# Soft-capped attention into soft-routed experts: k as plain fp32 transfers, w1 in whole rows, one raw V buffer

## The chip, the cores and the metric

The kernel runs on one core of a Trainium2 chip. The metric is the device time of one execution in microseconds; several executions give a median. The core has a matmul engine (TensorE, PE in the profile), a vector engine (VectorE, DVE), an activation engine (ScalarE, ACT), a general one (GpSimd, POOL) and SyncE (SP), which here only issues transfers. Matmuls write to PSUM, a small memory beside the working memory SBUF. Transfers between the chip's main memory and SBUF run on sixteen DMA engines; those that GpSimd issues show in queue q0, those of SyncE in q1.

## What is computed

Attention over 8 batches of 12 heads, 448 tokens of 64 elements each, with a soft cap on the scores, feeds a layer of 8 experts with 4 slots each.

```python
scores = scale * np.matmul(q, k.transpose(0, 1, 3, 2))
scores = cap * np.tanh(scores / cap)
attn = np.exp(scores - max); attn = attn / (sum + 1e-09)
x = (attn @ v), heads side by side           # (3584, 768)
logits = x @ phi                             # phi: (768, 32)
d = softmax of logits over the tokens
slot_input = d.T @ x                         # 8 experts x 4 slots x 768
h = np.maximum(slot_input[e] @ w1[e], 0.0)   # w1[e]: (768, 1024)
slot_out[e] = h @ w2[e]                      # w2[e]: (1024, 768)
out = (softmax of logits over the slots) @ slot_out
```

q, k, v, w1 and w2 are fp32 in main memory: 11 MB each for q, k and v, 25 MB for each of the weights.

## The kernel before

**Quads.** The attention goes in 24 quads Q of four heads each, three to a batch. A quad has two pairs n; the two heads h of a pair lie in the two halves of the 128 partitions. The 448 tokens of a head are seven columns of 64, so that token 7p + c is row p of column c. A head's keys make three and a half blocks of 128; the half blocks of both heads of a pair form one "mixed" tile. So a quad has 14 score tiles of 128 keys by 448 queries (`TILES`), made in six chunks (`CHUNKS`).

**A quad's steps**, by the names that the plan uses:
- `L`, `X`: q and k are loaded by GpSimd's queue, 224 KB each, with the cast from fp32 to bf16 in the transfer (`load`, L394), into two buffers each.
- `LV`, `XV`: V is loaded as fp32 by SyncE's queue in four transfers (`load_v`, L401) into one of two buffers `vraw`. `VC` casts it on GpSimd to `vb` (L406); `VS` writes a scaled copy `vw` on VectorE (L409). Both have two buffers.
- `T`, `C`: TensorE turns q and k by transposes of 64 columns (`turn`, L464), VectorE copies them out of PSUM (L470, L473), and the keys of the mixed tile into a block-diagonal `km` (L479).
- `SC`, `TH`: score matmuls (L494 mixed, L497) and the tanh on ScalarE (L507).
- `EX`: the exponential of eight tiles on ScalarE (L515). The six others are made on VectorE as a sum of four terms, `PH` (L528).
- `PV`: the products with V (`pv_mms`; L537, L540, L544), `NR` the division by the sums (L576, L577), `TX`, `CX` the turn of the result (L588, L592) for the logits.

Each quarter of the queries is 128 wide but the last, which is 64. The second head of a pair takes its queries in another order than the first, with the last column ahead, so that its odd quarter comes at the front. In the kernel before, the turned q holds eight columns, the last one twice, and each head reads seven of them. The mixed tile reads the seven of the first head's order for both; its products with V are then 130 wide, for both heads at once, but for the odd quarter, which VectorE first copies out for both heads into a block-diagonal tile `mt` (`MT`, L521).

**Weights.** While the attention runs, GpSimd's queue also loads w1 (32 parts of 384 KB) and w2 (32 parts), cast to bf16. All of w1 and the first `KEPT = 6` parts of w2 stay in SBUF. The other 26 parts of w2 go to a scratch in main memory (`w2d`) and are loaded again by SyncE once the attention gives its buffers free (`w2t`, L863).

**The order** of every engine's work is written out ahead by a list scheduler, `Plan`. It knows for each step an engine, an estimated duration (`COST`), the steps that it waits for and a due time, which the tables `DUE` and `HOLD` shift by name; the transfers are engines of their own, `DMA` for GpSimd's queue and `DMV` for SyncE's. Engines in `strict` take their steps in order of due time alone. The parts of the weights are spaced evenly over the plan. Each engine carries out its list in order and waits where an operand or a buffer isn't ready.

**After the attention** come the last batch's logits (to L855), the first layer (L886), the second layer (L917) in two halves, and the output, 11 MB, from L952 on.

Of the kernel before, what the change touches and what calls it, by code (L numbers as in the profile page):

```python
# [34 lines left out]
MIXED = slice(2, 8, 5)  # L35
# [7 lines left out]
ND_LAST = 4  # L43
FULL, ROWS, COLS, QUARTERS = range(4)
# [5 lines left out]
DUE = {"C0k": -10345, "C0q": -334861, "CAk": -123110, "CAq": -67932, "CE": -38879, "CN": -191711, "CS": -129158,  # L50
# [7 lines left out]
HOLD = {"C0q": 995, "CAk": 880, "CAq": 166, "CE": 267, "CN": 1500, "CS": 655, "CW": 848, "CX": 780, "Cq": 538, "ED":  # L58
# [5 lines left out]
COST = dict(quad=9000, lat=200, dma=4000, form=90, sc=100, scm=200, act=0.833, act0=70, ts=0.265, ts0=70,  # L64
            pvf=31, mixed=190, mtail=62, turn=430, xturn=410, copy=610, norm=830, vcast=1060, vscale=340, mcopy=220, kdiag=300,
            issue=800, load=1400, part=2050, same=300)


class Plan:
# [11 lines left out]
    def build(self):  # L81
# [11 lines left out]
        for Q in range(1, NQ):  # L93
            for n, nm in enumerate("kq"):
                t0 = Q * T - (2600, 1800)[n]
                op(("L", nm, Q), "POOL", C["issue"], [("T", nm, Q - 2)], t0 - 1.3 * T)
                op(("X", nm, Q), "DMA", C["load"], [("L", nm, Q)], t0 - 1.3 * T)
                op(("T", nm, Q), "PE", C["turn"] + 60 * n, [("X", nm, Q)], t0, take=True, form=(COLS, COLS))
                op(("C", nm, Q), "DVE", C["copy"] + (C["kdiag"], 90)[n], [("T", nm, Q), ("SC", Q - 2, nc - 1)], t0 + 400,
                   give=("T", nm, Q))  # L100
        for Q in range(NQ):
# [16 lines left out]
            op(("LV", Q), "SP", 1600, [("VC", Q - 2), ("VS", Q - 2)], t0 - 1.5 * T)  # L118
# [20 lines left out]
            op(("MT", Q), "DVE", C["mcopy"], [("EX", Q, 0), ("PV", Q - 2, "a1"), ("PV", Q - 2, "d")], te - 1, port=True)  # L139
            op(("PV", Q, "a0"), "PE", 24 * C["pvf"], [("EX", Q, 0)] + vs, te, take=True)  # L140
            op(("PV", Q, "a1"), "PE", C["mixed"] + C["mtail"], [("PV", Q, "a0"), ("MT", Q)], te + 1)
# [3 lines left out]
            op(("PV", Q, "d"), "PE", C["mixed"] + C["mtail"], [("MT", Q)] + vs, td - 10, take=True)  # L145
# [42 lines left out]
    def order(self):  # L188
# [3 lines left out]
        strict = ("ACT", "DMA", "DMV", "SP")  # L192
# [57 lines left out]
def kernel(  # L250
# [26 lines left out]
    KEPT = 6  # L277
# [14 lines left out]
    wide = consts.tile([P, 3 * P], BF16, name="ones")  # L292
    ones = wide[:, 0:P]
# [6 lines left out]
    pool.memset(wide[:, P:3 * P], 1.0)  # L300
# [26 lines left out]
    def load_w1(e, jh, fh):  # L327
# [10 lines left out]
    wjobs = [(load_w1, e, jh, fh) for e in range(E) for jh in range(2) for fh in range(2)]  # L338
# [12 lines left out]
    for nm in ("ld", "vr0", "qk0", "vr1", "ea0", "qk1", "ed0", "vb0", "ea1", "tm", "ed1", "vb1"):  # L351
        homes[nm] = att.enter_context(tc.tile_pool(name=nm, bufs=1))
# [4 lines left out]
    vraw = [homes[f"vr{n}"].tile([P, 2, SLOTS, DH], F32, name=f"vraw{n}") for n in range(2)]  # L357
# [3 lines left out]
    mt = [homes[f"vb{n}"].tile([P, 2, P], BF16, name=f"mt{n}") for n in range(2)]  # L361
# [6 lines left out]
    for t in (*mt, *km):  # L368
        dve.memset(t, 0.0)
# [27 lines left out]

    def load_v(Q):
        at = vraw[Q % 2].rearrange("p n (h t) d -> p n h (t d)", h=2)
# [5 lines left out]
    def vcast(Q):  # L405
        pool.tensor_copy(vb[Q % 2][:, :, :, 0:DH], vraw[Q % 2])  # L406

    def vscale(Q):
        dve.tensor_scalar(vw[Q % 2][:, :, 0:DH], vraw[Q % 2][:, 1, :, :], w_low, None, ALU.mult)  # L409

    first = {}
    TURN = {"k": [0, 4, 1, 5, 2, 6, 3], "q": [NT - 1] + list(range(NT))}
# [17 lines left out]
    def new_qkT(nm, Q):  # L430
        qkT[nm, Q] = homes[f"qk{Q % 2}"].tile([P, 2, (NT - 1 if nm == "k" else NT + 1), HP], BF16, name=nm + "T",
                                               tag=nm + "T", bufs=1)
        return qkT[nm, Q]
# [6 lines left out]
    def first_turn(nm, n, x0, x1, bank, at0):  # L440
        for x in range(x0, x1):
            for h in range(2):
                r = slice(h * HP, h * HP + HP)
                pe.transpose(bank[r, at0 + x - x0, :], casts[nm, n][r, TURN[nm][x], :], ident[r, r])

# [9 lines left out]
    def t0(nm):  # L455
        banks0[nm] = xbank(bank_of["T0", nm], [P, len(TURN[nm]), HP], BF16, name=nm + "p0")
        first_turn(nm, 1, 0, len(TURN[nm]), banks0[nm], 0)

    def turn(nm, Q):
        src = raws.pop((nm, Q))  # L460
        ps = xbank(bank_of["T", nm, Q], [P, 2, len(TURN[nm]), HP], BF16, name=nm + "ps")
        for x, c in enumerate(TURN[nm]):
            for h in range(2):
                pe.transpose(ps[h * HP:h * HP + HP, :, x, :], src[:, h, c * DH:(c + 1) * DH], ident)  # L464
# [23 lines left out]
    def qk_chunk(Q, s):  # L488
        for u in range(CHUNKS[s]):
# [3 lines left out]
            if h is None:  # L493
                pe.matmul(dst, km[Q % 2][:, n, :], qT[:, 1:NT + 1], start=True, stop=True)  # L494
            else:
                r = slice(h * HP, h * HP + HP)
                pe.matmul(dst, kT[r, 2 * t:2 * t + 2, :], qT[r, 1 - h:NT + 1 - h], start=True, stop=True)  # L497
# [19 lines left out]
    def mixed_tails(Q):  # L517

        for h in range(2):
            r = slice(h * HP, h * HP + HP)  # L520
            dve.tensor_copy(mt[Q % 2][r, :, r], rows(ea[Q % RQ])[r, MIXED, TAIL:S])  # L521

# [8 lines left out]
    def pv_mms(Q, dst, buf, vt, tiles, u0, begin=False, end=False):  # L531
        for g in range(NG):
            for x in tiles:
                n, h, t = TILES[x]
                q0 = (x - u0) * ROW + (g * P if not h else g * P + HP if g < NF else -HP)
                if h is not None:
                    pe.matmul(dst[:, 2 * g + h if g < NF else 2 * g, :], buf[:, q0:q0 + P], vt[:, 5 * h + t, :],  # L537
                              start=begin, stop=end, skip_group_check=True)
                elif g < NF:
                    pe.matmul(dst[:, 2 * g:2 * g + 2, :], buf[:, q0:q0 + P], vt[:, 3:5, :], start=begin,  # L540
                              stop=end, skip_group_check=True)
                else:
                    for h in range(2):
                        pe.matmul(dst[:, 2 * g, :], mt[Q % 2][:, n, :], vt[:, 3 + h, :], start=False, stop=end,  # L544
                                  skip_group_check=True)
                begin = False
# [4 lines left out]
    def pv(Q, what):  # L551
# [7 lines left out]
        if what == "a0":  # L559
            pv_mms(Q, dst, a, va, of(0, 0, NA), 0, begin=True)  # L560
        elif what == "a1":
            pv_mms(Q, dst, a, va, of(0, 0, NA, True), 0, end=True)
        elif what == "d":
            pv_mms(Q, dst, a, vd, of(1, 0, NA, True), 0, begin=True)
        elif what == "e":
            pv_mms(Q, dst, d, vd, of(1, NA + nd, NQT), NA)
        else:
            i = int(what[1])
            pv_mms(Q, dst, term_home(Q, i), vd if TERMS[i][1] == 1.0 else vw[Q % 2], range(NA, NA + nd), NA,
# [123 lines left out]
    def busy(n, home, by=None):  # L693
        by = ones if by is None else by
        if home.shape[-1] > P:
            for _ in range(n // 3):
                pe.matmul(home, ones, wide, start=True, stop=True)
# [7 lines left out]
        "C0": lambda nm: first_copy(nm, 1, 0, len(TURN[nm]), banks0.pop(nm), 0, dve),  # L705
        "L": load, "T": turn, "C": turned, "SC": qk_chunk, "TH": tanh_chunk, "LV": load_v,
        "VC": vcast, "VS": vscale, "MT": mixed_tails, "PH": term, "PV": pv, "EX": exp_tiles, "TX": x_turn, "CX": x_turned,
# [8 lines left out]

    load_first()
    load_v(0)
    for nm in "kq":
        load(nm, 1)  # L720
# [337 lines left out]
```

## Time and profile before

| | us |
|---|---|
| median of three runs | 301.25 |
| lowest and highest | 299.21, 301.88 |
| the profiled execution | 302.47 |
| its span, first to last instruction | 300.7 |

| engine | busy us | share of the span |
|---|---|---|
| TensorE | 257.6 | 86% |
| ScalarE | 234.9 | 78% |
| VectorE | 215.4 | 72% |
| GpSimd | 127.9 | 43% |

A group's row in the profile shows the line, the engine, the operation, the tiles written and read with their shapes, the count, the busy time, the mean of one instruction in ns, and behind the bar the idle time of the engine just before, with what ended it. Matmuls overlap each other, so that TensorE's busy time says little of its room. A queue's share is the time of its packets against sixteen engines over the stretch; packets of two queues can overlap, so shares add to more than 1. GB/s counts bytes written, and a cast from fp32 to bf16 writes half of what it reads.

### The profile page before, as it was taken

The numbers are of one execution on the slowest core, as the hardware profiler recorded it, in microseconds if no ns is written. First come the engines' busy times: TensorE is split into PE (matmuls) and PEld (weight loads), VectorE is DVE, ScalarE is ACT, GpSimd is POOL, SyncE is SP. The second block draws the span as 40 slices with busy tenths as digits, with TensorE's granted clock in tenths as the row PEclk, the third lists the DMA queues.
The fourth block names the chain that finished last, engine by engine and source line by source line (L and its number), as shares of the span: only waits on it lengthen the run. The fifth ranks groups of instructions, "written<-read, shape, count | busy, mean of one in ns | idle before, by whom it ended". The sixth has DMA issues, their size and how long they took to land.

```text
span 300.7 us, 11856 instructions
## 1 busy us (share of the span) xinstructions
PE 257.6 (86%) x5206; PEld 189.6 (63%) x5206; DVE 215.4 (72%) x465; ACT 234.9 (78%) x207; POOL 127.9 (43%) x188
## 2 busy tenths in 40 slices
PE   4789999499979999998998989897999989997610
PEld 4367678367766777677775767676677767543300
DVE  3378999179876987898687869875698786257730
ACT  2699999379986999899897989898799994236610
POOL 4644936536650765356634663476062200300000
PEclk9999999779997999999999999999799999999975
DMA  7978999999999999999999999999999799978995
GB/s 148 191 108 178 187 220 208 224 214 218 222 224 211 217 224 225 213 214 222 223 216 211 219 223 216 217 207 209 206 160 215 197 322 305 402 277 323 413 412 231
DMA packets 65203, 69.70 MB, mean 232 GB/s; under 512 B 4992, under 2 KB 60416, under 8 KB 65152
## 3 DMA queue, kind: packets, MB, share of 16 engines
q0 software_dynamic: 42992, 35.77, 75.9%
q1 hardware_dynamic: 22000, 32.94, 33.7%
q8 instruction: 41, 0.67, 0.8%
q10 hardware_dynamic: 160, 0.23, 0.3%
q14 instruction: 10, 0.08, 0.1%
HBM read 93.68 MB, written 21.23 MB: 382 GB/s over the span
## 4 chain that ended last, share of the span: by engine, by line
PE 55%; DMA 15%; ACT 12%; issue 6%; DVE 5%; SPq 2%; POOL 1%; DVEq 0%; ACTq 0%; POOLq 0%
PE pv L537 21%; PE sc L497 9%; DMA w1b<-in_moe_w_dram 8%; ACT exa L515 5%; ACT exa L507 3%; PE qps L464 3%; ACT exd L507 3%; PE sc L494 3%; PE kps L464 3%; PE xps L588 3%; DMA vraw<-in_v_dram 2%; PE pv L540 2%; DMA raw<-in_q_dram 2%; DMA out_dram<-ob 2%; PE so_ps L917 2%
## 5 line engine op out<-in xcount | busy, mean ns | idle before, releaser
L507 ACT ACTIVATE exa<-sc 128x1344 f16<-128x1344 f32 (+1 forms) x72 | 82.7, 1175 | 13.5 <-PE sc L497 9.1
L515 ACT ACTIVATE exa<-exa 128x3584 bf16<-128x3584 f16 x24 | 76.9, 3202 | 0.0
L507 ACT ACTIVATE exd<-sc 128x896 f16<-128x896 f32 x72 | 64.5, 924 | 12.0 <-PE sc L497 11.9
L528 DVE TENSOR_SCALAR term<-exd 128x2688 uint16<-128x2688 f16 (+1 forms) x72 | 62.0, 877 | 1.6 <-PE pv L537 1.2
L537 PEld LDWEIGHTS <-term 128*128 128x128 bf16 x1704 | 56.4, 97 | 8.0 <-issue 4.6
L497 PE MATMUL sc<-qT,kT 64*128 64x448 bf16 x288 | 51.2, 376 | 2.5 <-ACT exa L507 0.9
L537 PE MATMUL pv<-vb,term 128*128 128x65 bf16 x1136 | 43.2, 194 | 0.6 <-DVE term L528 0.3
L394 POOL DMA_DIRECT2D qb<-in_q_dram x23 | 17.3, 754 | 45.3 <-PE sc L497 32.7
L394 POOL DMA_DIRECT2D kb<-in_k_dram x23 | 18.2, 790 | 38.4 <-PE sc L497 34.2
L577 DVE TENSOR_TENSOR xq<-pv,rec 128x448 bf16<-128x448 f32 (+2 forms) x49 | 30.1, 615 | 1.7
L331 POOL DMA_DIRECT2D w1b<-in_moe_w_dram x32 | 26.5, 829 | 8.8 <-DMA w1b<-in_moe_w_dram 6.5
L406 POOL CAST vb<-vraw 128x1024 bf16<-128x1024 f32 x24 | 26.5, 1106 | 7.5 <-issue 4.1
L537 PE MATMUL pv<-vb,exa 128*128 128x65 bf16 x576 | 24.0, 200 | 3.0 <-issue 2.4
L537 PEld LDWEIGHTS <-exa 128*128 128x128 bf16 x576 | 21.5, 102 | 4.6 <-issue 3.0
L537 PE MATMUL pv<-vw,exd 128*128 128x65 bf16 x568 | 22.4, 196 | 2.0 <-issue 2.0
L629 POOL COPY e<-E 128x512 bf16<-128x512 bf16 x9 | 5.8, 641 | 42.2 <-ACT E L822 18.2
L473 DVE COPY qT<-qps 128x1024 bf16<-128x1024 bf16 x23 | 15.7, 684 | 10.1 <-PE qps L464 10.0
L537 PE MATMUL pv<-vw,term 128*128 128x65 bf16 x568 | 21.7, 193 | 1.2 <-issue 1.2
L335 POOL DMA_DIRECT2D w2d<-in_moe_w_dram x26 | 21.8, 853 | 0.0
L537 PEld LDWEIGHTS <-exd 128*128 128x128 bf16 x576 | 19.7, 99 | 3.1 <-issue 2.2
L528 DVE TENSOR_SCALAR exd<-exd 128x2688 uint16<-128x2688 f16 (+1 forms) x24 | 20.8, 868 | 0.8
L497 PEld LDWEIGHTS <-kT 64*128 64x128 bf16 x288 | 12.8, 94 | 13.3 <-issue 4.9
(143 smaller groups left out, 377.7 us busy)
## 6 DMA issues: line engine op xcount, KB each, us to landing
w1b<-in_moe_w_dram POOLq DMA_DIRECT2D x32, 384.0 KB, 14.2
w2d<-in_moe_w_dram POOLq DMA_DIRECT2D x26, 384.0 KB, 12.1
w2t<-w2d SPq DMA_DIRECT2D x26, 384.0 KB, 6.0
out_dram<-ob SPq DMA_DIRECT2D x9, 768.0 KB, 8.6
vraw<-in_v_dram SPq DMA_DIRECT2D x48, 128.0 KB, 6.5
kb<-in_k_dram POOLq DMA_DIRECT2D x23, 224.0 KB, 10.0
qb<-in_q_dram POOLq DMA_DIRECT2D x23, 224.0 KB, 10.2
vraw<-in_v_dram SPq DMA_DIRECT2D x48, 96.0 KB, 6.5
```

Source lines behind the costliest of these rows:

```text
L331: pool.dma_start(out=w1b[e][:, js, fs], in_=w1r[:, e, js, fs])
L335: pool.dma_start(out=dst, in_=bass.AP(tensor=src.tensor, offset=src.offset + half * HD, ap=[[D, P], [F * D, 4], [1, HD]]))
L394: pool.dma_start(out=t, in_=bass.AP(tensor=srcs[nm].tensor, offset=quad_at(Q), ap=[[NT * DH, P], [2 * S * DH, 2], [1, NT * DH]]))
L406: pool.tensor_copy(vb[Q % 2][:, :, :, 0:DH], vraw[Q % 2])
L464: pe.transpose(ps[h * HP:h * HP + HP, :, x, :], src[:, h, c * DH:(c + 1) * DH], ident)
L473: dve.tensor_copy(new_qkT(nm, Q), ps)
L497: pe.matmul(dst, kT[r, 2 * t:2 * t + 2, :], qT[r, 1 - h:NT + 1 - h], start=True, stop=True)
L507: act.activation(quad_ex(Q, u0, u0 + w).bitcast(F16), ring(Q, s)[:, 0:w, 0:S], ACT.Tanh, scale=qk_scale / cap)
L515: act.activation(t, t.bitcast(F16), ACT.Exp, scale=cap)
L528: dve.tensor_scalar(rows(term_home(Q, i))[:, 0:nd, 0:S].bitcast(U16), quad_ex(Q, NA, NA + nd).bitcast(F16), octaves * 128, base[i], ALU.mu ...
L537: pe.matmul(dst[:, 2 * g + h if g < NF else 2 * g, :], buf[:, q0:q0 + P], vt[:, 5 * h + t, :], start=begin, stop=end, skip_group_check=True)
L577: dve.tensor_tensor(xq[Q][:, s0:s1, n, :], ps[:, s0:s1, 0:DH], rec.to_broadcast([P, s1 - s0, DH]), op=ALU.mult)
```

## The change

Five things change together, and the plan is made anew with other tables.

1. k is loaded by SyncE as plain fp32 (448 KB) into one buffer `kraw`, and VectorE casts it into one buffer `kcast` (new steps `LK`, `XK`, `KC`). The load of quad Q waits for the cast of Q-1; the cast of Q waits for the turn of Q-1.
2. w1 comes in 24 parts of 512 KB, two blocks of 128 rows in their whole length of 1024, where it came in 32 parts of 384 KB, three blocks in half their length.
3. The second head's queries are turned in their own order, so that the turned q has seven columns and 14 transposes where it had 16. The mixed tile now holds the two heads' queries in different orders; its products with V are made per head, eight of ordinary width, and `mt` with its copies goes.
4. One buffer `vraw` for V in place of two: the load of quad Q waits for the casts of Q-1, where it waited for those of Q-2.
5. Eight parts of w2 stay in SBUF and 24 are reloaded. The room comes from the V buffer, `mt` and the wide tile of ones.

The plan's steps on `SP` and `DMV` are no longer strict, the weights' parts get their own durations, and they are spread over one quad more.

```diff
+    op(("LK", Q), "SP", 400, [("KC", Q - 1)], t0 - 1.3 * T)
+    op(("XK", Q), "DMV", C["load"], [("LK", Q)], t0 - 1.3 * T)
+    op(("KC", Q), KCAST, C["kcast"] if KCAST == "DVE" else 950, [("XK", Q), ("T", nm, Q - 1)], t0 - 0.5 * T, port=True)
...
-            op(("LV", Q), "SP", 1600, [("VC", Q - 2), ("VS", Q - 2)], t0 - 1.5 * T)
+            op(("LV", Q), "SP", 1600, [("VC", Q - 1), ("VS", Q - 1)], t0 - 1.5 * T)
...
-            op(("MT", Q), "DVE", C["mcopy"], [("EX", Q, 0), ("PV", Q - 2, "a1"), ("PV", Q - 2, "d")], te - 1, port=True)
...
-            t = 3000 + k * (NQ * T - 2 * T) / self.parts
+            t = 3000 + k * (NQ * T - T) / self.parts
             op(("W", k), "POOL", C["issue"], (), t, after=t)
-            op(("XW", k), "DMA", C["part"], [("W", k)], t)
+            op(("XW", k), "DMA", C["part1"] if k < 24 else C["part2"], [("W", k)], t)
...
-        strict = ("ACT", "DMA", "DMV", "SP")
+        strict = ("ACT", "DMA")
...
-    KEPT = 6
+    KEPT = 8
...
-        js, fs = slice(3 * jh, 3 * jh + 3), slice(512 * fh, 512 * fh + 512)
-        pool.dma_start(out=w1b[e][:, js, fs], in_=w1r[:, e, js, fs])
+        js = slice(2 * jh, 2 * jh + 2)
+        pool.dma_start(out=w1b[e][:, js, :], in_=w1r[:, e, js, :])
...
+    def load_k(Q):
+        sp.dma_start(out=kraw, in_=bass.AP(tensor=k.tensor, offset=quad_at(Q),
+                                           ap=[[NT * DH, P], [2 * S * DH, 2], [1, NT * DH]]))
+
+    def cast_k(Q):
+        (dve if KCAST == "DVE" else pool).tensor_copy(kcast, kraw)
+        raws["k", Q] = kcast
...
-    TURN = {"k": [0, 4, 1, 5, 2, 6, 3], "q": [NT - 1] + list(range(NT))}
+    TURN = {"k": [[0, 4, 1, 5, 2, 6, 3]] * 2, "q": [[*range(NT)], [NT - 1, *range(NT - 1)]]}
...
-                pe.matmul(dst, km[Q % 2][:, n, :], qT[:, 1:NT + 1], start=True, stop=True)
+                pe.matmul(dst, km[Q % 2][:, n, :], qT, start=True, stop=True)
...
+                n, a, t = TILES[x]
+                for h in range(2) if a is None else (a,):
+                    q0 = (x - u0) * ROW + (g * P if not h else g * P + HP if g < NF else -HP)
+                    pe.matmul(dst[:, 2 * g + h if g < NF else 2 * g, :], buf[:, q0:q0 + P],
+                              vt[:, 3 + h if a is None else 5 * h + t, :],
                               start=begin, stop=end, skip_group_check=True)
...
     load_first()
+    load_k(1)
     load_v(0)
-    for nm in "kq":
-        load(nm, 1)
+    load("q", 1)
```

More of the change, by code (lines that the diff above doesn't have):

```diff
@@ L43 @@
 ND_LAST = 4
+KCAST = "DVE"
 FULL, ROWS, COLS, QUARTERS = range(4)
@@ L48 @@
 PH = len(TERMS)
-DUE = {"C0k": -10345, "C0q": -334861, "CAk": -123110, "CAq": -67932, "CE": -38879, "CN": -191711, "CS": -129158,
[7 rows of a table removed]
-HOLD = {"C0q": 995, "CAk": 880, "CAq": 166, "CE": 267, "CN": 1500, "CS": 655, "CW": 848, "CX": 780, "Cq": 538, "ED":
[5 rows of a table removed]
-COST = dict(quad=9000, lat=200, dma=4000, form=90, sc=100, scm=200, act=0.833, act0=70, ts=0.265, ts0=70,
-            pvf=31, mixed=190, mtail=62, turn=430, xturn=410, copy=610, norm=830, vcast=1060, vscale=340, mcopy=220, kdiag=300,
-            issue=800, load=1400, part=2050, same=300)
+DUE = {"C0k": -50037, "C0q": -404649, "CAk": -142919, "CAq": -143270, "CE": -32285, "CN": -365487, "CS": -113014,
[7 rows of a table added]
+HOLD = {"C0k": 1500, "C0q": 1052, "CAk": 720, "CAq": 52, "CE": 739, "CN": 697, "CW": 223, "Cq": 749, "ED": 1313,
[3 rows of a table added]
+COST = dict(quad=9000, lat=200, dma=3000, form=90, sc=100, scm=200, act=0.833, act0=70, ts=0.265, ts0=70,
+            pvf=31, turn=430, xturn=410, copy=610, norm=830, vcast=1060, vscale=340, kcast=540, kdiag=300,
+            issue=800, load=1400, part1=2740, part2=2530, same=300)
 class Plan:
@@ L95, in build @@
                 t0 = Q * T - (2600, 1800)[n]
[L96 to L99, printed above, removed]
+                if nm == "k":
+                    op(("LK", Q), "SP", 400, [("KC", Q - 1)], t0 - 1.3 * T)
+                    op(("XK", Q), "DMV", C["load"], [("LK", Q)], t0 - 1.3 * T)
+                    op(("KC", Q), KCAST, C["kcast"] if KCAST == "DVE" else 950, [("XK", Q), ("T", nm, Q - 1)], t0 - 0.5 * T, port=True)
+                else:
+                    op(("L", nm, Q), "POOL", C["issue"], [("T", nm, Q - 2)], t0 - 1.3 * T)
+                    op(("X", nm, Q), "DMA", C["load"], [("L", nm, Q)], t0 - 1.3 * T)
+                op(("T", nm, Q), "PE", C["turn"], [("X", nm, Q), ("KC", Q)][1 - n:2 - n], t0, take=True, form=(COLS, COLS))
+                op(("C", nm, Q), "DVE", C["copy"] + (C["kdiag"], 0)[n], [("T", nm, Q), ("SC", Q - 2, nc - 1)], t0 + 400,
                    give=("T", nm, Q))
@@ L144, in build @@
             td = t0 + T + 1200
[L145 removed]
+            op(("PV", Q, "d"), "PE", 8 * C["pvf"], [("EX", Q, 0)] + vs, td - 10, take=True)
             for i in range(PH):
@@ L290 @@
     psT = ctx.enter_context(tc.tile_pool(name="psT", bufs=1, space=PSUM))
-    wide = consts.tile([P, 3 * P], BF16, name="ones")
-    ones = wide[:, 0:P]
+    ones = consts.tile([P, NS], BF16, name="ones")
     dve.memset(ones, 1.0)
@@ L356 @@
     terms_of = [homes["tm"].tile([P, ND * ROW], BF16, name=f"term{n}") for n in range(RP)]
-    vraw = [homes[f"vr{n}"].tile([P, 2, SLOTS, DH], F32, name=f"vraw{n}") for n in range(2)]
+    kraw = homes["ld"].tile([P, 2, S], F32, name="kraw")
+    kcast = homes["ld"].tile([P, 2, S], BF16, name="kcast")
+    vraw = homes["vr"].tile([P, 2, SLOTS, DH], F32, name="vraw")
     vb = [homes[f"vb{n}"].tile([P, 2, SLOTS, W], BF16, name=f"vb{n}") for n in range(2)]
@@ L851 @@
     for a in range(0, P, NS):
-        pe.matmul(junk[a:a + NS, :], ones[:, 0:NS], wide, start=True, stop=True,
+        pe.matmul(junk[a:a + NS, :], ones, w2b[:, 0, 0, :], start=True, stop=True,
                   skip_group_check=True)
```

91 lines of the change are left out of this document (35 added, 56 removed), and 22 rows, old and new, of tables (DUE, HOLD).

## The prediction

> **What bounds the kernel now.** I read the windows first, to see which stretch the time is in; then ScalarE's timeline and its waits, for what the long stretch lacks; then the transfer queues of the same stretch, and the chain.
>
> The kernel handles 24 quads (four heads each). The eight-tile exponentials of ScalarE (L515), one per quad, are a good ruler:
>
> ```profile
> 15.96 3.20 ACT L515 ACTIVATE exa<-exa 128x3584 bf16<-128x3584 f16 x1
> 42.79 3.20 ACT L515 ACTIVATE exa<-exa 128x3584 bf16<-128x3584 f16 x1
> 60.81 0.92 ACT L507 ACTIVATE exd<-sc 128x896 f16<-128x896 f32 x1 [5.54 <-PE sc L497]
> 245.68 3.20 ACT L515 ACTIVATE exa<-exa 128x3584 bf16<-128x3584 f16 x1
> ```
>
> ```profile
> core 0: us, PE busy (x) PEld busy (x) DVE busy (x) ACT busy (x) POOL busy (x), PEclk, DMA share, GB/s
> 15.96:42.79 26.83, 25.69 (x526) 19.42 (x525) 23.57 (x47) 26.54 (x23) 15.32 (x18) 1.00 0.96 170
> 42.79:245.68 202.89, 186.69 (x4026) 144.06 (x4023) 160.62 (x342) 179.33 (x149) 100.12 (x131) 0.97 1.21 217
> 98.61:107.50 8.89, 8.89 (x211) 7.13 (x208) 8.52 (x18) 8.77 (x8) 5.83 (x8) 1.00 1.23 217
> 245.68:300.70 55.02, 35.33 (x564) 20.11 (x560) 25.67 (x49) 21.34 (x29) 2.97 (x3) 0.89 0.89 337
> ```
>
> The first three quads take 26.83/3 = 8.94 us each, with ScalarE busy for 26.54 of 26.83. The next twenty take 202.89/20 = 10.14 each, with ScalarE busy for 179.33, or 8.97 a quad. So the exponentials would allow 9 us, and 22.8 us are lost in that stretch; ScalarE's waits there name the same 22.8, all on score matmuls:
>
> ```profile
> ACT exd L507 <- PE sc L497: 11.9, 10, 5.5
> ACT exa L507 <- PE sc L497: 8.0, 8, 1.4
> ACT exa L507 <- PE sc L494: 2.9, 8, 0.6
> ```
>
> What differs between the two stretches is the DMA share, 0.96 against 1.21. The queues of the long stretch alone (packets, MB, share of 16 engines; then count, KB each, median us to landing):
>
> ```profile
> q0 software_dynamic: 38108, 32.03, 99.5%
> q1 hardware_dynamic: 11771, 11.36, 20.4%
> ...
> vraw<-in_v_dram SPq DMA_DIRECT2D x36, 128.0 KB, 6.7
> kb<-in_k_dram POOLq DMA_DIRECT2D x18, 224.0 KB, 10.3
> ```
>
> q0 carries everything that GpSimd issues: k, q and both weights. Its packets alone fill 99.5% of sixteen engines. The longest stall shows how this reaches the matmuls; in the chain of waits:
>
> ```profile
> 39.77 15.85 DMA w1b<-in_moe_w_dram
> ...
> 56.15 0.74 POOL kb L394
> 56.89 0.63 POOL e L629
> ...
> 57.57 0.36 PE zps L636 x4
> ```
>
> GpSimd stood before a k issue until a w1 transfer had landed, the copy e queued behind it, TensorE waited for e, and ScalarE lost 5.54 us.
>
> **The change, part by part.** The profiled execution took 302.47 us: 300.70 of span and 1.77 around it. It lies 1.22 above the median of the three runs, 301.25; the sum below is made against 302.47 and then lowered by 1.22.
>
> Vector and GpSimd work, from the groups of instructions:
>
> ```profile
> L406 POOL CAST vb<-vraw 128x1024 bf16<-128x1024 f32 x24 | 26.5, 1106 | 7.5 <-issue 4.1 <-DMA vraw<-in_v_dram 2.7 <-PE pv L537 0.4
> L394 POOL DMA_DIRECT2D kb<-in_k_dram x23 | 18.2, 790 | 38.4 <-PE sc L497 34.2 <-PE pv L544 1.9 <-DMA w1b<-in_moe_w_dram 1.7
> L473 DVE COPY qT<-qps 128x1024 bf16<-128x1024 bf16 x23 | 15.7, 684 | 10.1 <-PE qps L464 10.0
> L592 DVE COPY xT<-xps 128x896 bf16<-128x896 bf16 x23 | 14.3, 621 | 2.6 <-PE xps L588 2.2
> L521 DVE COPY mt<-exa 64x128 bf16<-64x128 bf16 x48 | 10.7, 223 | 3.4 <-ACT exa L515 3.0
> L437 DVE CAST casts<-raw 128x448 bf16<-128x448 f32 x2 | 0.8, 394 | 1.0 <-DMA raw<-in_q_dram 0.8 <-DMA raw<-in_k_dram 0.2
> L437 DVE CAST casts<-raw 128x192 bf16<-128x192 f32 x1 | 0.3, 253 | 0.0
> ```
>
> *The cast of k* is new: 128x896 from fp32. The two L437 rows give (394-253)/256 = 0.55 ns an element, so 394 + 448 x 0.55 = 641 ns, 23 times. *Removed* are two mt copies a quad, 2 x 223 = 446 ns, and the q copy shrinks from 1024 to 896 columns, 684 to about 621 (the xT row), 63 ns. Net +0.13 us a quad on VectorE, which is busy for 160.62/20 = 8.03 of 10.14: nothing, unless VectorE becomes the bound (below). GpSimd loses 23 issues of 790 ns, and eight w1 issues; it was busy for half of the stretch, so the gain is only that e and the V cast no longer queue behind k.
>
> TensorE, from the chain:
>
> ```profile
> 65.17 0.73 PE pv L537 x24
> ...
> 66.19 0.57 PE qps L464 x16
> ...
> 67.06 0.51 PE kps L464 x14
> ...
> 249.84 0.17 PE pv L540 x3
> 250.02 0.06 PE pv L544 x2
> ```
>
> Fourteen q transposes in place of sixteen: 0.57 to 0.51. Each mixed tile had three wide products and two tails, 0.17 + 0.06 = 0.23; now eight ordinary ones at 0.73/24, 0.24. Twice a quad: -0.06 + 0.02, taken as nothing.
>
> *w1 in whole rows and eight resident w2 parts.* The bytes read stay the same, in 24 transfers of 512 KB for 32 of 384; fewer packets in q0 is worth between nothing and what half of w1's packets cost, and is on no path of its own: 0. Two of 26 reloads go:
>
> ```profile
> 235.86 25.11 SPq L863 DMA_DIRECT2D w2t<-w2d  x26
> ```
>
> That is 2 x 25.11/26 = 1.9 us of SyncE's queue, hidden: in the chain the second layer follows on the first without a transfer between. 0, or -1.9 if that cover were not there. At the start k of quad 1 goes to SyncE's queue ahead of V of quad 0; the first V cast did not wait for its transfer, so 0.
>
> *One V buffer* is the edit that I think decides. Before, load_v(Q) waited for the casts of Q-2; now for vcast and vscale of Q-1, and these can't run before their own load has landed. So there is a closed turn in each quad: issue of four transfers, landing, cast, next issue. It has a measured example, where the buffer of two quads before was just as late:
>
> ```profile
> 18.22 0.60 SPq L401
> ...
> 20.16 7.40 DMA vraw<-in_v_dram
> ```
>
> ```profile
> 27.72 1.30 POOL L406 CAST vb<-vraw 128x1024 bf16<-128x1024 f32 x1 [2.68 <-DMA vraw<-in_v_dram]
> ```
>
> ```profile
> 29.04 1.76 SPq L401 DMA_DIRECT2D vraw<-in_v_dram  x2
> ```
>
> From the first issue at 18.22 to the next load that this cast released, 29.04: 10.82 us, the upper end. The lower end uses medians of the long stretch: 1.94 from first to last issue, 6.7 to landing, 0.16 (27.56 to 27.72), 1.11 for a cast, 0.02: 9.93. I take 10.2, nearer to the medians, as they come from the twenty quads that count. Both ends are above 8.97, and on either side of today's 10.14.
>
> *k in V's queue* adds to that turn when its transfer stands in front of V's. It has 256 packets, 16 an engine. A q1 packet took 0.204 x 202.89 x 16/11771 = 56 ns at 965 bytes, so some 104 at 1792; and a q0 packet, 0.995 x 202.89 x 16/38108 = 85 ns, may go in between: 16 x 189 ns = 3.0 us. If the two fall at random in a 10.2 us turn, k is in flight at V's issue in 3.0/10.2 of the quads, with half of it left: 0.44 us a quad, 8.8 in all; 0 if k always stands behind. I take the middle, 4.4. The queue that k leaves is freed by 16 x 85 ns = 1.4 us a quad, the other takes up as much.
>
> Sum: 42.79 + 20 x 10.2 + 4.4 + 55.02 + 1.77 = 308.0, less 1.22: **307**. Its own range: 42.79 + 198.6 + 56.79 - 1.22 = 297 to 42.79 + 216.4 + 8.8 + 56.79 - 1.22 = 324.
>
> **The rivals.**
>
> *The queue is relieved and V comes sooner (faster).* k leaves the queue that was full. If q0 then has gaps, V lands in less than 6.7 us; from 5.5 us on the turn is under 8.8 us and decides nothing. Then the stall at 60.81 goes, and with it some of the small ones. Gone stall 5.54 and half of the other 22.8 - 5.54 = 17.3: 14.2 us, 302.47 - 14.2 - 1.22 = 287. For it: 99.5% was q0's alone. Against it: shorter quads mean that the same bytes are asked for in less time.
>
> *Nothing that counts has moved (same).* k's bytes are read as before, only q1's share grows by what q0's shrinks; the sum of both, 1.20, stays, and with it 10.14 us a quad: 301. The Trainium skill (DMA: Bandwidth & Descriptors, section Issuing engines are not separate DMA queues) says that transfers issued by SyncE and by GpSimd run on the same 16 engines, so that a change of the issuing engine saves only the time of issuing. By that rule alone the answer is this rival's; the two shares, which add to more than 1, agree only in part.
>
> *Longer w1 packets hold V up (much slower).* If each V packet waits for one q0 packet, and w1's are twice as long, a V load of 512 packets, 32 an engine, takes 32 x 85 ns = 2.7 us longer while w1 is loaded. The new plan spaces its parts by 23 x 9000/56 = 3696 ns of quads of 9000, so the 24 parts of w1 span ten quads, some eight of them in the long stretch: 307 + 22 = 329. The Trainium skill (same page, section Queues, rings and completion order) says that an engine takes turns between its queues a packet at a time; no run here shows yet what a packet of that row length does.
>
> *VectorE becomes the bound.* In the fast quad at 98.61 it was busy for 8.52 of 8.89 us; 0.13 more would show there. 20 x 0.13 = 2.6 us: 304.
>
> **The numbers.** What a measurement of this kernel tells from no change is about 1%, 3 us. The V turn sets the pace: 0.50, of which 0.33 is slower by more than 1%, 0.12 within, 0.05 faster. Relief: 0.35, faster. Nothing moved: 0.05. Long w1 packets: 0.08, slower. VectorE: 0.02, slower. Together faster 0.40, same 0.17, slower 0.43. The range leaves out a tenth at either end: below it a relief that ends nearly all 22.8 us of waiting (278), above it the long packets. 286 to 321.
>
> **What would show it.** The V turn: the four V issues should follow VectorE's or GpSimd's cast at once in every quad, the casts should wait for vraw's landing (2.7 us in all before, some 20 then), and the ruler's spacing should be 10 us or more with vraw at 6.5 us or more to landing. The relief: spacing near 9.3, q0 well under 99%, vraw landing in 5 us, no wait of GpSimd before e. If the casts don't wait for V, the step on the single buffer is wrong, whatever the time is. VectorE as the bound would show as ScalarE and TensorE waiting for kT, qT or term.

## The result, and the profile after

| | before | after |
|---|---|---|
| median of the runs, us | 301.01 (4 runs) | 337.84 (4 runs) |
| lowest and highest | 299.21, 301.88 | 334.89, 341.85 |
| the profiled execution | 302.47 | 334.89 |
| its span | 300.7 | 333.1 |

The ratio is 1.120, with an interval of 1.108 to 1.132: 12% slower. The ratios here and below leave out runs more than 1.5% above the fastest of their kernel (here 341.85), so they can differ a little from the ratio of the medians. The prediction said 307, in a range of 286 to 321. The mechanism on which it bet came true and its size did not; the direction was near luck, with chances of 0.43 for slower and 0.40 for faster.

The windows of after, cut like those of before: the start, up to the fourth long exponential of ScalarE, the next twenty quads, and the rest. The columns are the time, the busy times of the engines with their instruction counts, the granted clock, the DMA share and GB/s.

```profile
14.43:53.70 39.27, 28.69 (x520) 21.50 (x519) 24.42 (x43) 26.71 (x22) 13.00 (x15) 0.87 1.01 210
53.70:279.17 225.47, 193.97 (x4121) 149.16 (x4118) 166.25 (x322) 180.81 (x149) 86.63 (x107) 0.92 1.01 198
279.17:333.10 53.93, 36.04 (x575) 20.68 (x571) 25.55 (x47) 22.13 (x30) 2.97 (x3) 0.92 0.92 354
```

ScalarE's work is what it was: 26.71 us at the start (26.54 before) and 180.81 in the long stretch (179.33). The three stretches end at 53.70 (42.79 before: 10.9 later), take 225.47 (202.89: 22.6 more) and 53.93 (55.02: 1.1 less), 32.4 us together. So a third of the loss is in the first three quads, where the prediction had none, and a long quad takes 11.27 us in place of 10.14.

The DMA engines are not busier but idler in the long stretch, 1.01 against 1.21. The queues of that stretch (packets, MB, share of 16 engines), and its issues (count, KB each, median us from issue to landing):

```profile
q0 software_dynamic: 25891, 24.89, 71.1%
q1 hardware_dynamic: 17099, 19.16, 29.0%
...
kraw<-in_k_dram SPq DMA_DIRECT2D x18, 448.0 KB, 8.5
vraw<-in_v_dram SPq DMA_DIRECT2D x40, 128.0 KB, 6.2
```

q0 is down from 99.5 to 71.1%, and yet V's transfers land after 6.2 us, hardly sooner than the 6.7 before. What has changed is who waits for them. The waits of the whole execution (engine, line, what was waited for; us in all, times, the longest):

```profile
POOL vb L415 <- DMA vraw<-in_v_dram: 97.5, 15, 10.0
ACT exa L518 <- PE sc L505: 32.9, 27, 5.8
DVE vw L418 <- DMA vraw<-in_v_dram: 32.1, 14, 5.4
PEld L542 <- DVE term L533: 22.7, 18, 6.1
ACT exd L518 <- PE sc L508: 21.7, 14, 6.6
...
DVE kcast L404 <- DMA kraw<-in_k_dram: 17.1, 10, 3.0
```

GpSimd's cast waited 2.7 us for V in all of before and waits 97.5 now; VectorE, which had no such wait among its larger ones, stands for 32.1 us before vw and 17.1 before kcast. One such wait shows the way to ScalarE. First VectorE's timeline (start, us, engine, line; in brackets the idle time ahead and what ended it), then ScalarE's:

```profile
68.89 0.61 DVE L591 COPY xT<-xps 128x896 bf16<-128x896 bf16 x1
74.91 0.43 DVE L418 TENSOR_SCALAR vw<-vraw 128x512 bf16<-128x512 f32 x1 [5.41 <-DMA vraw<-in_v_dram]
75.26 1.70 DVE L533 TENSOR_SCALAR term<-exd 128x2688 uint16<-128x2688 f16 x1
```

```profile
79.04 0.92 ACT L518 ACTIVATE exd<-sc 128x896 f16<-128x896 f32 x1 [6.55 <-PE sc L508]
79.86 3.18 ACT L526 ACTIVATE exa<-exa 128x3584 bf16<-128x3584 f16 x1
```

VectorE reached vw at 69.5 and stood there until V had landed. The term, whose inputs do not depend on this V, stands behind it in the list and began 5.4 us late; TensorE's products wait for the term, the score matmuls stand behind the products, and ScalarE lost 6.55 us. The same landing in the chain of waits:

```profile
63.64 0.60 SPq L410
64.24 0.04 issue
64.28 10.51 DMA vraw<-in_v_dram
74.79 0.02 issue
74.81 0.04 POOLq L415
74.86 0.09 issue
74.94 1.30 POOL vb L415
76.25 0.02 issue
76.27 0.60 SPq L410
```

Landing, cast, and 0.02 us later the next load: the closed turn that the prediction described, though with 10.51 us of landing. Further on, the chain goes through k in the same way:

```profile
152.41 8.84 DMA kraw<-in_k_dram
161.25 0.02 issue
161.27 0.74 DVE kcast L404
162.01 0.08 DVE rec L575
162.09 9.28 DMA kraw<-in_k_dram
171.37 0.02 issue
171.39 0.63 DVE kcast L404
```

### The profile page after: what moved, and what is told of

Read it like the earlier page. It is cut to its first block, busy times and chain, and to the rows that moved or that the text cites. A ratio compares the mean times of both kernels' runs of the same rounds, so it can differ in the third digit from the quotient of the medians.

```text
span 333.1 us, 11972 instructions
## 1 busy us (share of the span) xinstructions
PE 268.0 (80%) x5300; PEld 197.2 (59%) x5300; DVE 221.7 (67%) x437; ACT 236.5 (71%) x207; POOL 108.7 (33%) x154
## 4 chain that ended last, share of the span: by engine, by line
DMA 44%; PE 25%; DVE 12%; SPq 6%; ACT 4%; issue 3%; POOL 2%; DVEq 0%; POOLq 0%; ACTq 0%
DMA kraw<-in_k_dram 26%; DMA vraw<-in_v_dram 17%; PE pv L542 10%; SPq L410 6%; PE sc L508 3%; DVE term L533 3%; DVE kcast L404 2%; POOL vb L415 2%; PE so_ps L912 2%; PE hp L879 2%; PE kps L475 1%; DMA raw<-in_q_dram 1%; DVE vw L418 1%; PE op L1004 1%; DVE ob L1011 1%
## 5 line engine op out<-in xcount | busy, mean ns | idle before, releaser
L542 PEld LDWEIGHTS <-term 128*128 128x128 bf16 x1704 | 62.1, 102 | 26.0 <-DVE term L533 22.7
L415 POOL CAST vb<-vraw 128x1024 bf16<-128x1024 f32 x24 | 28.8, 1198 | 147.7 <-DMA vraw<-in_v_dram 97.5
L533 DVE TENSOR_SCALAR term<-exd 128x2688 uint16<-128x2688 f16 (+1 forms) x72 | 65.5, 930 | 1.6 <-PE pv L542 0.7
L542 PE MATMUL pv<-vb,term 128*128 128x65 bf16 x1136 | 48.0, 203 | 17.6 <-DVE term L533 17.4
L542 PE MATMUL pv<-vb,exa 128*128 128x65 bf16 x960 | 43.6, 197 | 3.1 <-ACT exa L526 0.7
L542 PEld LDWEIGHTS <-exa 128*128 128x128 bf16 x960 | 37.5, 100 | 11.8 <-issue 8.5
L418 DVE TENSOR_SCALAR vw<-vraw 128x512 bf16<-128x512 f32 x24 | 12.0, 500 | 32.2 <-DMA vraw<-in_v_dram 32.1
L404 DVE CAST kcast<-kraw 128x896 bf16<-128x896 f32 x23 | 16.3, 708 | 17.2 <-DMA kraw<-in_k_dram 17.1
L575 DVE RECIPROCAL rec<-pv 128x7 f32<-128x7 f32 (+2 forms) x49 | 9.7, 198 | 18.4 <-PE pv L542 18.2
L331 POOL DMA_DIRECT2D w1b<-in_moe_w_dram x24 | 19.1, 798 | 0.1
L508 PEld LDWEIGHTS <-kT 64*128 64x128 bf16 x288 | 13.1, 94 | 9.6 <-issue 2.7
```

Of the source, the lines that this page charges most:

```text
L331: pool.dma_start(out=w1b[e][:, js, :], in_=w1r[:, e, js, :])
L404: (dve if KCAST == "DVE" else pool).tensor_copy(kcast, kraw)
L415: pool.tensor_copy(vb[Q % 2][:, :, :, 0:DH], vraw)
L508: pe.matmul(dst, kT[r, 2 * t:2 * t + 2, :], qT[r], start=True, stop=True)
L533: dve.tensor_scalar(rows(term_home(Q, i))[:, 0:nd, 0:S].bitcast(U16), quad_ex(Q, NA, NA + nd).bitcast(F16), octaves * 128, base[i], ALU.mu ...
```

## The experiments

Each ratio is to runs of the kernel before on the same chip, in the same session.

**Are the single buffers the cause?** Doubling them needs room, so five w2 parts stay resident in place of eight. The first kernel prices that alone.

```diff
-    KEPT = 8
+    KEPT = 5
```

> The kernel after with five instead of eight parts of w2 resident and nothing else, the base for the next three, which need the room: the lists of all engines up to the end of the attention are the same. Every theory: the attention stays as it is (24 quads at about 11.5 us, 338 us in all), and three more reloads cost 0 to 3 us at the end: 337 to 342.

Measured: 341.33 us, ratio 1.135 (1.126 to 1.144). Against after's 1.120 (1.108 to 1.132) that is 3.5 us or nothing; the next three are compared with it.

```diff
+    vraw = [homes["vr"].tile([P, 2, SLOTS, DH], F32, name=f"vraw{n}") for n in range(2)]
...
+        at = vraw[Q % 2].rearrange("p n (h t) d -> p n h (t d)", h=2)
...
```

> Two raw V buffers in the changed kernel, five w2 parts resident, every engine's list as before: only the wait of the V load for the casts of the quad before goes. Turns (each quad waits for the round of load and cast of its single buffers): the V round is gone, the k round stays, and as k no longer shares its time with a late V it falls from 11.7 us to about 10: 320, and GpSimd's wait for vraw falls from 97 us to under 20. Long rows (w1's packets of 2 KB hold every SyncE transfer up, buffers or not): the loads stay at 8 us and more and the waits with them: 332 or more.

Measured: 313.89 us, 1.044 (1.029 to 1.059). V's second buffer is worth 27 us; GpSimd's wait for V fell from 97.5 us in after to 28.7. The lists are the same as in after.

```diff
+    kraw = [homes["ld"].tile([P, 2, S], F32, name=f"kraw{n}") for n in range(2)]
...
+        (dve if KCAST == "DVE" else pool).tensor_copy(kcast, kraw[Q % 2])
...
```

> Two raw k buffers in the changed kernel, five w2 parts resident, lists unchanged; the V buffer stays single. Turns: the V round of about 11 us stays and sets the pace: 325 to 335, VectorE's wait for kraw (17 us) gone, its wait for vraw still over 20. If the k round is the one that counts: 315 or less. Long rows: 332 or more.

Measured: 339.05 us, 1.127 (1.114 to 1.140). k's second buffer alone is worth 2 us, within the scatter.

> Two raw buffers for V and for k, five w2 parts resident, lists unchanged. Turns: neither round is closed, VectorE and GpSimd no longer wait for vraw or kraw, and the quads fall to 9.2 to 9.6 us: 288 to 300. Long rows: the two loads still take 8 us and more, over 315.

Both edits together: 301.78 us, 1.003 (0.999 to 1.007). So 40 us go, where the two alone give 27 and 2: the turns stand side by side, and with V's undone k's is the next, worth 12. Without the two single buffers the whole loss is gone. What didn't come is the gain of the relieved queue: the doubled kernel stands where before stood.

**Is it V's buffer alone, or k's bytes in the same queue?** Before, with one vraw; each V load is put behind the two casts of the quad before, and all else keeps its order.

```diff
-    vraw = [homes[f"vr{n}"].tile([P, 2, SLOTS, DH], F32, name=f"vraw{n}") for n in range(2)]
+    vraw = [homes["vr0"].tile([P, 2, SLOTS, DH], F32, name="vraw0")] * 2
...
```

> The kernel before with one V buffer and nothing else changed: same lists, but each V load stands behind the two casts of the quad before. Theory A, one V buffer alone makes the long turn: 23 turns of 11.3 us as in the changed kernel, 42.8 + 20 x 11.3 + 56 = 325 us. Theory B, my prediction's turn without k in the queue, 9.9 to 10.8 us: 297 to 316, most likely 305 us; vb's wait for vraw some 20 to 40 us in all. Theory C, V alone is hidden and only both together are long: 301 us.

Measured: 329.66 us, 1.094 (1.084 to 1.104). One V buffer alone, with k still in GpSimd's queue, costs 28 us. A piece of its chain (here L401 issues V, L406 casts it):

```profile
136.51 0.60 SPq L401
...
139.36 5.21 DMA vraw<-in_v_dram
...
144.72 1.31 POOL vb L406
146.05 0.59 SPq L401
...
148.38 7.58 DMA vraw<-in_v_dram
```

and the first and last start of its long exponentials:

```profile
L515 ACT ACTIVATE exa<-exa x24: 3182/3200/3206, 16.2 to 272.7; 128x3584 bf16<-128x3584 f16 x24
```

(272.7 - 16.2)/23 = 11.15 us a quad, near after's 11.51 and theory A's 11.3, and not as in my sum (10.2).

**Do the long w1 packets hold V up?** In the trace's records, each of which is one row, a q0 packet of w1 takes 98 ns where it writes 1 KB (before) and 172 where it writes 2 KB (after), in the median. Here the 24 parts are kept, in rows of 512:

```diff
-        js = slice(2 * jh, 2 * jh + 2)
-        pool.dma_start(out=w1b[e][:, js, :], in_=w1r[:, e, js, :])
+        for js, fh in ((slice(0, 4), jh),) if jh < 2 else ((slice(4, 6), 0), (slice(4, 6), 1)):
+            fs = slice(512 * fh, 512 * fh + 512)
+            pool.dma_start(out=w1b[e][:, js, fs], in_=w1r[:, e, js, fs])
```

> The changed kernel with w1's rows cut in halves of 512 again (24 parts as before, 1-KB packets on the SBUF side; a part's third third goes as two transfers). V turns measured 12.1 us a quad while w1 is loaded and 10.6 while w2 is. Theory A, long w1 packets hold V and k up: the turn of the w1 stretch falls to the other's 10.6, ten turns x 1.5 us, so about 323 us and vraw's landing shorter there. Theory B, the turn is long because k and V share one queue and each has one buffer, whatever runs beside them: 335 to 341 us, the same 12 us turns in the w1 stretch.

Measured: 327.34 us, 1.082 (1.068 to 1.097): 10 us of after's 37. Three landings of V in its chain, then those of after at the same quads:

```profile
29.89 7.81 DMA vraw<-in_v_dram
...
60.59 6.52 DMA vraw<-in_v_dram
70.52 7.47 DMA vraw<-in_v_dram
```

```profile
32.17 9.91 DMA vraw<-in_v_dram
...
64.28 10.51 DMA vraw<-in_v_dram
78.21 8.09 DMA vraw<-in_v_dram
```

They are 2.1, 4.0 and 0.6 us shorter. Over quads 1 to 10, while w1 is loaded, the mean landing is 7.2 us against 8.4 in after, and the V turn 10.8 against 12.1. That is about what it is while w2 is loaded (10.7 and 10.6), as theory A had it. V has 512 packets a quad, 32 an engine; if each waits for one w1 packet, 32 x (172 - 98) ns = 2.4 us is the estimate, twice the mean difference. The Trainium skill (DMA: Bandwidth & Descriptors, section Queues, rings and completion order) says that an engine changes between its queues only at the end of a packet; its packet holds several descriptors, so that the wait of one row for one row is not what it states, and no run here shows at which grain the engines change.

The same rows in the kernel before, where V has two buffers:

```diff
-    wjobs = [(load_w1, e, jh, fh) for e in range(E) for jh in range(2) for fh in range(2)]
+    wjobs = [(load_w1, e, jh) for e in range(E) for jh in range(3)]
...
```

> The kernel before with w1 in 24 parts of whole rows, nothing else changed but the duration of a part in the plan. Theory A, long packets only cost where a closed turn waits for V: with two V buffers nothing, 299 to 303 us. Theory B, they also hold up k and q in their own queue: 5 to 11 us more, 306 to 312.

Measured: 302.98 us, 1.011 (1.006 to 1.016). About 3 us, nearer to nothing than to 10: long packets cost mainly where somebody waits for each load. And short rows in the doubled kernel:

> Two buffers each for V and k, five w2 parts resident, and w1 in rows of 512 again; else the changed kernel. Theory A, with the buffers doubled nobody waits for a single transfer and the row length is worth nothing: 300 to 303 us. Theory B, shorter packets let V and k land sooner even so: 293 to 298 us, the best of both kernels.

Measured: 305.02 us, 1.020 (1.011 to 1.028), 3 us above the doubled kernel with whole rows (by the ratios 1.7%, or 5 us). So there whole rows cost nothing; why short ones should cost anything, these runs don't tell.

**Are the lists to blame?** The plan reckoned with 3 us from the end of SyncE's issue to the landing (that of before with 4). Told 7, it puts the casts later, behind work that can run:

```diff
-                t = max(t, end[d] + (0 if x == o["eng"] else COST["dma"] if x[0:2] == "DM" else lat))
+                t = max(t, end[d] + (0 if x == o["eng"] else {"DMA": 3000, "DMV": 7000}[x] if x[0:2] == "DM" else lat))
...
```

> The changed kernel, with the plan told that a transfer of SyncE's queue lands 7 us after its issue ends where the table had 3 us; nothing else is changed, so the casts stand later in the lists of VectorE and GpSimd. Theory A, the closed turns of V and k set the pace themselves: no gain, 333 to 345 us, with fewer waits of TensorE for term. Theory B, the turn is 10 us and the rest of the loss is work queued behind casts that stand too early in the lists: 312 to 322 us.

Measured: 356.69 us, 1.189 (1.176 to 1.202), worse than either theory had it. TensorE no longer waits much for term, but a cast that stands later is a next load that is issued later: both casts were done 3.2 us after the landing in the mean, 1.6 in after, and the V turn is 12.1 us against 11.1. Neither place tried in the list is right with one buffer: early, the cast blocks what is behind it; late, it lengthens the turn.

The same care with both buffers doubled: the plan is told that a load, of V or of k, waits for the casts of two quads before.

```diff
-            op(("LV", Q), "SP", 1600, [("VC", Q - 1), ("VS", Q - 1)], t0 - 1.5 * T)
+            op(("LV", Q), "SP", 1600, [("VC", Q - 2), ("VS", Q - 2)], t0 - 1.5 * T)
...
```

> Two buffers each for V and k, five w2 parts resident, and the plan told of it: a load waits for the casts of the quad two before, so the issues move ahead in SyncE's list. Theory A, with the buffers doubled only the reading of main memory is left as the pace, some 10 us a quad as before: 299 to 303 us. Theory B, late issues in the old list still cost it: q0 is down at 62 percent, so quads of 9.3 us are possible and the time is 287 to 295 us.

Measured: 304.14 us, 1.010 (1.006 to 1.014). Earlier issues gain nothing over 301.78.

**Why does V take so long to land?** Between the last w1 part and the resident w2 parts, 23 of 24 transfers of w2 are left out:

```diff
-    wjobs += [(load_half, w2d[part], *part) for part in w2_spilled]
+    wjobs += [(load_half, w2d[part], *part) if n == 0 else (lambda: None,) for n, part in enumerate(w2_spilled)]
...
```

> The changed kernel without 23 of the 24 transfers of w2 to the scratch (they are left out, and the reloads all read the one part that is there), so that q0 carries only q between the last w1 part, some 140 us in, and the eight resident parts, which stay in their places some 215 us in. Theory A, V's landing is long because its packets share the engines with the weights': with q idle at the start it was 2.3 us from the last issue to the last packet, against 6.8 later, so the V turn of that stretch falls from 10.6 us to 6 to 8 and decides nothing any more; the quads there take 9.0 to 9.4 us, and some nine of them give 11 to 15 us: 322 to 327. Theory B, the turn is long by the issues, k ahead in the same queue and the casts: the turn stays over 10 us, 335 to 340 us.

Measured: 323.31 us, 1.079 (1.075 to 1.083), in theory A's range. Its windows, six quads with w1 beside and nine with almost no weights beside, and V's issues in the stretch from 148 to 229 us:

```profile
62.90:143.82 80.92, 61.92 (x1223) 47.41 (x1220) 50.33 (x99) 54.57 (x46) 27.60 (x35) 0.85 0.92 187
154.02:234.71 80.69, 80.37 (x1862) 63.29 (x1859) 73.22 (x147) 80.07 (x68) 21.53 (x30) 1.00 0.61 132
```

```profile
vraw<-in_v_dram SPq DMA_DIRECT2D x19, 128.0 KB, 4.2
```

The first stretch holds 6 quads (80.92/6 = 13.5 us each) and the second 9 (80.69/9 = 8.97 us each) with ScalarE busy for 80.07 of 80.69: with one buffer each, and V landing in 4.2 us, the closed turns decide nothing. It is the weights beside them that make the turn longer than ScalarE's quad.

**And why does the doubled kernel gain nothing?** The same omission with both buffers doubled (26 of its 27 transfers):

> Both buffers doubled, five w2 parts resident, and 26 of the 27 transfers of w2 to the scratch left out, so that q0 carries little but q from some 140 to 215 us in. It asks why the doubled buffers stay at 9.9 us a quad though q0 fell from 99 to 62 percent. Theory A, main memory is read at its pace: about 390 GB/s stand in the records whenever weights are due, by q0 and q1 together, so it does not matter which queue k is in; without the weights the quads of that stretch go at 9.0 us, eight of them, 295 us or less. Theory B, the lists or the fetching of instructions set 9.9 us: no change, 300 to 303.

Measured: 291.58 us, 0.968 (0.961 to 0.976). Its windows, with w1 beside and without weights, from the longest of its three executions, 294.74 us:

```profile
46.06:136.28 90.22, 81.34 (x1855) 63.40 (x1852) 74.61 (x147) 80.62 (x68) 32.99 (x43) 1.00 1.06 229
136.28:216.97 80.69, 80.27 (x1862) 63.19 (x1859) 72.30 (x147) 80.08 (x68) 22.15 (x28) 1.00 0.57 131
```

Nine quads each: 10.02 us with w1 beside, 8.97 without. The doubled kernel with its w2 transfers, over a stretch of nearly the same time and length:

```profile
136.00:217.00 81.00, 73.95 (x1701) 57.82 (x1698) 66.52 (x133) 73.00 (x61) 34.63 (x45) 1.00 1.17 223
```

ScalarE got 73.00 us of work done in 81.00 there and 80.08 in 80.69 here. The lists and buffers of the two kernels are the same but for those transfers and their issues on GpSimd, so it is w2's transfers that cost the tenth us with k in SyncE's queue. Before has the same tenth us with k in GpSimd's; no run leaves the weights out there.

The traces show where the time goes, and it is not a V or k that somebody waits for. TensorE's own waits, first in the doubled kernel from 136 to 217 us, then without w2 from 136.28 to 216.97:

```profile
PE pv L542 <- issue: 4.1, 5, 1.1
PE qps L475 <- issue: 1.6, 1, 1.6
PE zps L635 <- DVE term L533: 0.9, 1, 0.9
PE qps L475 <- DMA qb<-in_q_dram: 0.3, 1, 0.3
```

```profile
PE sc L507 <- ACT exd L517: 0.2, 1, 0.2
```

"issue" is idle time for which the profile shows no releaser; here it is 5.7 of the 7.05 us for which TensorE stood. Each of the six pauses ended 2.2 to 2.4 us after a packet of 16 KB had started in q8, the queue that the profile calls "instruction". The same holds for the twelve pauses over 0.3 us in before between 17 and 245 us, 10.8 us in all (2.3 to 2.5 us after such a packet). So TensorE seems to stand for its own instructions, which come late while weights are loaded: theory B's fetching, but set by theory A's weights. This is read from the times and no run tests it. A fixed pace of main memory does not show: with q0's bytes counted twice for the cast, before reads 389 GB/s from 46 to 136 us, and the doubled kernel 378 in about the same time and 346 from 136 to 217.

The Trainium skill (same page, section Issuing engines are not separate DMA queues) says that changing the issuer moves no work off the sixteen engines; here q0 lost k, and the time with both buffers doubled was 1.003 of before's.

**The rotated queries** alone, in before, with every list in its order:

```diff
-    TURN = {"k": [0, 4, 1, 5, 2, 6, 3], "q": [NT - 1] + list(range(NT))}
+    TURN = {"k": [[0, 4, 1, 5, 2, 6, 3]] * 2, "q": [[*range(NT)], [NT - 1, *range(NT - 1)]]}
...
```

> The kernel before with only the second head's queries turned in their own order: 14 transposes of q, eight ordinary products for a mixed tile, no mt and no copies to it; every list keeps its order. My prediction took it as nothing: 299 to 303 us. The other theory, 0.45 us a quad less on VectorE and no wait of TensorE for mt: 292 to 298 us.

Measured: 301.13 us, 1.004 (1.0005 to 1.008): at most some 2 us slower, and nothing gained, near what the prediction took it for.

**A version that beats both?** In the doubled kernel the second quad took 13.1 us, where TensorE waited for a q that landed at 18.6. It is issued ahead of the memsets:

```diff
     load("q", 1)
+    load("q", 2)
...
```

> Both buffers doubled, five w2 parts resident, and q of quad 2 issued beside q of quad 1, ahead of the memsets on GpSimd. In the doubled kernel the second quad took 13.1 us, against 9.0 before, with TensorE waiting for that q, which landed at 18.6 us. If that is all, the first three quads take 9 us each in place of 10.6 and the time falls by 3 to 5: 297 to 299 us, ahead of both kernels by a little. If V or k of quad 2 is just as late, nothing changes: 301 to 303.

Measured: 300.28 us, 0.9995 (0.996 to 1.003). The first three quads went from 10.6 to 9.7 us each, not to 9, and the rest did not follow. No kernel that does all the work beat before by more than can be told.

## Why the prediction was wrong

The steps of the sum, against the profiled execution (334.89, where the sum before its last correction said 308.0):

| step | forecast | measured | off by |
|---|---|---|---|
| end of the first three quads | 42.79 | 53.70 | 10.9 |
| twenty quads | 204.0 | 225.47 | 21.5 |
| k in V's queue | 4.4 | in the row above | -4.4 |
| the rest, and around the span | 56.79 | 55.72 | -1.1 |

**The V turn: the mechanism was right, its size wrong.** That it closes, that the casts wait for V, that the next four issues follow the cast at once, that the ruler's spacing is over 10 us: all of it is in the profile. Its terms in us, measured as means over the turns of quads 3 to 22:

| term of the turn | forecast | after | before with one V buffer |
|---|---|---|---|
| first to last issue | 1.94 | 2.18 | 2.13 |
| last issue to landing | 6.7 | 7.32 | 7.21 |
| landing to GpSimd's cast | 0.16 | 0.17 | 0.15 |
| the cast | 1.11 | 1.19 | 1.21 |
| VectorE's vw, where it ends after the cast | not counted | 0.21 | 0.39 |
| to the next issue | 0.02 | 0.06 | 0.04 |
| the turn | 9.93, taken as 10.2 | 11.13 | 11.13 |

The term that was most mis-sized is the landing, 6.7 us. It was the median of single transfers, while the cast waits for the last of four: counted from the last issue, the landings of one V buffer in before are mostly 6 to 8.5 us, and 4.6 to 10.5 in after. Counted in the same way, the trace that the prediction had shows 7.2 in the mean from 34 us on. The row beside it showed 7.40 in a stretch where q0 was not yet full (72.9%); I took that as part of the upper end, though it spoke for more where q0 is full. The smaller part is in the other terms; the next load waits for vw too, which ended after GpSimd's cast in 7 of the 20 turns. With one V buffer alone the pace is 11.15; my upper end was 10.82.

**The first three quads were left as they were.** The sum multiplied the new turn by twenty and kept 42.79. But the turn holds from the second quad on, as soon as w1 flows. One V buffer in before puts the fourth exponential at 48.98, 6.2 us late; whole w1 rows add to that: the changed kernel has it at 48.34 with short rows and at 53.70 with whole ones.

**w1 in whole rows was put at nothing**, as on no path of its own; the rival with long packets named the effect, got a chance of 0.08, and priced it at 2.7 us a V load (1.2 measured) and 22 us in all. Undone beside single buffers it gives 10, in before it costs some 3.

**k in V's queue** was priced as something that delays V, 4.4 us. No run shows that: the V turn is 11.1 us in before with one V buffer and k in the other queue, and 10.8 in the changed kernel with short rows. It mattered differently: k has a closed turn too, behind V's in the queue, 8.5 us to landing against the 3.0 that I worked out from packets alone. But while V's turn is the longer one, freeing k gives only 2 us; the 12 show when V is freed.

**The relief** had 0.35. Its condition, that q0 gets gaps, was met, 71% in after and 79% in the doubled kernel from 46 to 245 us (the 62% of two expectations is of its whole span, where before has 75.9%). V's landing with both buffers doubled was still not short, 7.4 us for 128 KB in that stretch; the weights' bytes are the same. What I counted for it, 99.5%, was one queue's share; the share of all, 1.21 before and 1.14 there, was the better row. And of the 15.5 us for which TensorE waited in the long stretch of before, only the 3.6 before zps came through q0 as I had told it; 11.5 were "issue". The rival "nothing moved", 0.05, is what the doubled buffers measured: 301.78.

**VectorE as the bound** did not come: 166.25 of 225.47 us busy. The sign named for it, TensorE waiting for term, came even so (18.4 us). What VectorE did is to stand still ahead of work that was ready, and this the prediction listed only for the casts themselves, not for the terms behind them. Of the small terms, TensorE at nothing was right as far as can be told, and the cast of k, 641 ns, measured 708.

What stays open: how V's landing becomes long beside the weights, by main memory or by the sharing of the engines, which no run here separates; and whether TensorE's pauses are waits for instructions.

## What to carry to other kernels

A buffer taken away turns issue, landing, cast and next issue into one closed loop; size it by the last of its transfers to land, at the load of the stretch where it will run, and from the first quad that has it. If that sum comes near the quad's own time, the waiting instruction also holds up whatever stands behind it on its engine, and neither of the two places tried in the list mended that. A queue that is full tells little about relief: look at the share of all queues together, and ask whether any bytes go away.

## What was not expected of the hardware

Landing depends on what is beside more than on size: V's transfers of 128 KB took 4.2 us with little but q and k beside them (one buffer, no w2) and 6.2 in after (k's 448 KB 4.7 and 8.5), and from the last issue up to 10.5 with w1 in long rows. A casting transfer's packet took 98 ns for 1 KB written and 172 for 2 KB in the median, so that the longer row saves 12% of the packet time (172 against 2 x 98); beside single buffers V landed 1.2 us later with it in the mean. The granted clock was 0.85 in the stretch with w1 beside single buffers, where TensorE was busy for 61.92 of 80.92 us, and 1.00 in the stretch with almost no weights of the same execution. TensorE's longest unexplained pauses came 2.2 to 2.5 us after 16-KB packets of the instruction queue in before and in the doubled kernel, and none came in the stretch without w2.
